# Loading the first head pair of queries and keys as f32 over the hardware queue, casting it on VectorE, and re-ordering the head of a fused attention and GEGLU kernel

## The chip, the cores and the metric

The kernel runs on one core of one Trainium2 chip. The metric is the device time of one execution in microseconds (us), as the median of several runs. Seven runs of the kernel before gave a median of 267.21 us, from 266.68 to 267.8 us.

The engines are called by the names of the profile: PE (TensorE matmul), PEld (TensorE weight load), DVE (VectorE), ACT (ScalarE), POOL (GpSimd) and SP (SyncE). PE, DVE and ACT each work through their own list of instructions in the order of the program. POOL issues the DMAs of the software queue [...], SP those of the hardware queue.

## What is computed

Inputs q, k and v have the shape (4 batches, 8 heads, 768 tokens, 64), in f32. Attention is sparse: a query sees the tokens less than 16 away, and besides them 24 block summaries, one for each block of 32 tokens. The output of attention goes through a GEGLU feed-forward part with a gated residual.

```python
k_sum = k.reshape(B, H, nb, block, D).max(axis=3)
v_sum = v.reshape(B, H, nb, block, D).mean(axis=3)
scores_l = where(|i - j| < 16, scale * q @ k.T, -1e9)
scores_s = scale * q @ k_sum.T + log(block)
a = softmax(concat([scores_l, scores_s]))
x = a @ concat([v, v_sum])              # heads side by side: (3072, 512)
ffn = (gelu(x @ w_gate) * (x @ w_val)) @ w_out
out = x + sigmoid(x @ w_res) * ffn      # d_ff = 1536
```

## The kernel before

Tokens are worked off in 8 units of 384 (half a batch each). A unit has an attention part and a feed-forward part. From unit to unit the two are interleaved: while the feed-forward part of unit u runs on PE, the scores and the attention of unit u+1 are woven in. The order of all instructions is written out by hand, and the loop over u (from L454) holds all of this. Only unit 0 has no feed-forward part to lie behind: its loads and its attention come first, alone, in the code of L124 to L160 (constants and loads) and L408 to L452. This piece is called the head here, and the change lies in it.

**The work of the head, by head pair.** There are four head pairs, hp = 0 to 3.

- `k_step` (L187) turns the keys of a pair on PE (16 small transposes at L183 into the PSUM tile `tp`), ACT copies them into the tile `kW` (L190), and `k_rest` (L194 to L203) makes five DVE instructions of them: two for the block maxima, two copies of the neighbouring tokens, one copy of the maxima.
- `q_step` (L205) turns the queries of a pair (8 transposes) and ACT copies them into `qT` (L207).
- `mask_step` (L249) writes the band mask into the PSUM tile `s` with two matmuls (L252), and `s_step` (L257) adds the scores on top with 12 small matmuls (L269). ACT takes the exponential (L278) into `P`. There is only one buffer for `s`, so that the mask of the next pair waits for the exponential of this one.
- `v_spread` (L235) are two DVE copies that lay the values out for odd tiles (L239, L242). `vsum_sum` (L221) sums values into block means with seven matmuls, one for each chunk of 128 tokens (L227); `vsum_out` (L231) copies the result out, two heads by DVE, six by ACT.
- `av_part` (L288) multiplies P with the values (L301): 12 matmuls with `blocks=False` for the tokens near by, 12 with `blocks=True` for the block means. `av_norm` (L304) divides by the row sum on DVE (L309, L311).
- `xt_step` (L313) turns the result for the feed-forward part: PE at L320, ACT copy at L322. The first feed-forward matmuls of unit 0 (tiles `gv`, `g`, `vv`, L333) follow.
- `keep_warm(n)` (L378) issues n matmuls on zeros (tile `wp`, L382) whose result nobody reads.

**Loads.** All loads of the head go over POOL's software queue in this order: keys of heads 0 to 3, queries of heads 0 to 3, keys of heads 4 to 7, queries of heads 4 to 7 (`load_tokens`, L85), then the seven chunks of the values (L96), then the weights `w_gate` and `w_val` in six slices each. Each has its type changed from f32 to bf16 on the way. Between them POOL makes masks with `select` (L115): `ident`, the bias, `maskt`, `bmean`. Eight of these DMAs may be under way at once; the ninth waits for the first.

**Order on PE in the head before:** 13 wp; k0, q0, k1, q1; mask, 3 wp, scores 0; k2, q2, mask, scores 1; k3, q3, mask, scores 2; value sums 0 to 2, 2 wp, mask, scores 3, 2 wp; value sums 3 to 6, each with 2 wp behind it (the last with 1); then near and block parts of pairs 0 and 1, then of 2 and 3; 3 wp; the turning of x.

**Order on DVE in the head before:** memsets of constants; `nmask` (L122), which needs `maskt` from POOL; memsets of `kW` and `vsum`; the four times five instructions of `k_rest`; the two `v_spread` copies; the copy out of the value sums; the norms.

Of the kernel before, what the change touches and what calls it, by code (L numbers as in the profile page):

```python
# [8 lines left out]
F32 = mybir.dt.float32  # L9
BF16 = mybir.dt.bfloat16  # L10
AF = mybir.ActivationFunctionType
# [4 lines left out]
def kernel(  # L16
# [11 lines left out]
    nc = tc.nc  # L28
    B, H, S, D = q.shape
# [12 lines left out]
    TU = S // 2  # L42
    NSUB = TU // 128
    NU = 2 * B
    NP = H // 2
    BAND = QT + 2 * WIN
    PP = 96

    const = ctx.enter_context(tc.tile_pool(name="const", bufs=1))
    wpool = ctx.enter_context(tc.tile_pool(name="wpool", bufs=1))  # L50
    qk = ctx.enter_context(tc.tile_pool(name="qk", bufs=2))
    work = ctx.enter_context(tc.tile_pool(name="work", bufs=3))
    ppool = ctx.enter_context(tc.tile_pool(name="ppool", bufs=4))
    upool = ctx.enter_context(tc.tile_pool(name="upool", bufs=2))
# [4 lines left out]
    MM, AO, TT, SS = (ps_mm, "mm"), (ps_o, "ao"), (ps_t, "t"), (ps_s, "s")  # L59
# [3 lines left out]
    NC = NT // 2  # L63
# [3 lines left out]
    bias_t = const.tile([128, 1], F32, name="bias_t")  # L67
    nmask = const.tile([128, QT], BF16, name="nmask")
    bmean = const.tile([128, NB - 2 + 128], BF16, name="bmean")
    pre = const.tile([1, 1], F32, name="pre")  # L70
# [9 lines left out]

    def token_tile(lo, hi, name):
        j = (hi - lo) // PP
        return qk.tile([PP, H, j, D], BF16, tag=f"{name}{j}", name=name)

    def load_tokens(t, src, b, lo, hi, h0, h1):  # L85
        j = (hi - lo) // PP
        nc.gpsimd.dma_start(  # L87
            out=t[:, h0:h1].rearrange("p h j d -> p h (j d)"),
            in_=src[b, h0:h1, lo:hi].rearrange("h (p j) d -> p h (j d)", j=j),
        )  # L90

    def load_values(b, c):

        lo, hi = (max(0, c * 128 - WIN), c * 128 + 128 - WIN) if c < NC else (S - WIN, S)
        dst = vext[b % 2][0 if c else WIN:128, 2 * c, :, 0:D] if c < NC else vext[b % 2][64:64 + WIN, NT - 1, :, 0:D]
        nc.gpsimd.dma_start(out=dst, in_=v[b, :, lo:hi, :].rearrange("h p d -> p h d"))  # L96

    k_sb, q_sb = {}, {}

    with tc.manual_schedule():  # L100

        def vext_consts(i):
            nc.vector.memset(vext[i][:, :, :, D:D + 1], 1.0)
            nc.vector.memset(vext[i][0:WIN, 0], 0.0)
            nc.vector.memset(vext[i][64:96, NT - 1], 0.0)
            nc.vector.memset(vext[i][64:64 + WIN, NT - 1, :, D:D + 1], 1.0)
# [7 lines left out]
        def select(ap, op, fill, base, step, cm):  # L114
            nc.gpsimd.affine_select(out=ap, in_=ap, compare_op=op, fill=fill, base=base,  # L115
                                    pattern=[[step, ap.shape[-1]]], channel_multiplier=cm)
# [9 lines left out]
        nc.vector.memset(bias_t[:], 0.0)  # L126
        nc.vector.memset(bias_t[96:128, :], logblk)
        nc.vector.memset(bmean[:], 1.0 / BLK)
        vext_consts(0)

        kt, qa, qb = token_tile(0, S, "k_sb"), token_tile(0, TU, "q_sb"), token_tile(TU, S, "q_sb")
        k_sb[0] = kt
        load_tokens(kt, k, 0, 0, S, 0, 4)
        select(ident[:], ALU.not_equal, 1.0, 0, -1, 1)
        load_tokens(qa, q, 0, 0, TU, 0, 4)
        load_tokens(kt, k, 0, 0, S, 4, 8)
        load_tokens(qa, q, 0, 0, TU, 4, 8)
        select(bias_t[96:128, :], ALU.is_ge, -30000.0, NB - 1, 0, -1)
        load_values(0, 0)
        mask_consts()  # L140
        kw_consts(0)
# [45 lines left out]
        def k_step(b, hp, pool, tag):  # L187
            tp = turn_pair(k_sb[b], hp, pool, tag)
            kw = kW[b % 2][hp]
            nc.scalar.copy(kw[:, :, OWN:OWN + QT].rearrange("d t (p j) -> d t p j", j=tp.shape[2]),  # L190
                           tp.rearrange("d (t p) j -> d t p j", t=NT))
            k_rest(kw)
# [12 lines left out]
        def q_step(src, b, lo, hi, hp, pool, tag):  # L205
            tp = turn_pair(src, hp, pool, tag)
            nc.scalar.copy(qT[b % 2][hp][:, lo:hi].rearrange("d (p j) -> d p j", j=tp.shape[2]), tp)  # L207
# [13 lines left out]
        def vsum_sum(b, pool, tag, chunks=range(NC + 1), vs=None):  # L221
            if vs is None:
                vs = pool.tile([128, DM], F32, tag=tag, name="vs")
            for c in chunks:
                lo = NB - 2 - 4 * c if c < NC else 0
                rows, t = (slice(0, 128), 2 * c) if c < NC else (slice(64, 64 + WIN), NT - 1)
                nc.tensor.matmul(vs[:], bmean[rows, lo:lo + 128], vext[b % 2][rows, t, :, 0:D],  # L227
                                 start=(c == 0), stop=(c == NC), skip_group_check=True)
            return vs
# [27 lines left out]
        def s_step(u, hp, st, s=None, two=None, masked=True):  # L257
            b, half = u // 2, u % 2
            first = s is not None
            if two:  # L260
                s = [pool.tile([128, 512], F32, tag=tag, name="s1") for pool, tag in two]
            elif not first:
                s = ps_s.tile([128, 2, 512], F32, tag="s", name="s")
            kw, qt = kW[b % 2][hp], qT[b % 2][hp]
            for t in range(HT):
                tt = half * HT + t
                for hh in range(2):
                    ps = slice(hh * 64, hh * 64 + 64)
                    nc.tensor.matmul((s[hh] if two else s[:, hh])[:, t * QT:(t + 1) * QT], kw[ps, tt, :],  # L269
                                     qt[ps, tt * QT:(tt + 1) * QT], start=not first, stop=True,  # L270
                                     skip_group_check=True)
            P = ppool.tile([128, 2, HT, QT], BF16, tag="P", name="P")
            if two:
                for hh in range(2):
                    nc.scalar.activation(P[:, hh].rearrange("p t q -> p (t q)"), s[hh][:, 0:TU], AF.Exp,  # L275
                                         scale=scale, bias=bias_t[:])
            else:
                nc.scalar.activation(P.rearrange("p a t q -> p a (t q)"), s[:, :, 0:TU], AF.Exp,  # L278
                                     scale=scale, bias=bias_t[:])
            st["P", hp] = P  # L280
            if not first and masked:
                mask_part(hp, st)
# [23 lines left out]
        def av_norm(hp, st):  # L306
            ao = st["ao", hp]
            rz = work.tile([128, NSUB, 2, 1], F32, tag="rz", name="rz")
            nc.vector.reciprocal(rz[:], ao[:, :, :, D:D + 1])  # L309
            xn = st["xn"].rearrange("p s (h d) -> p s h d", d=D)[:, :, 2 * hp:2 * hp + 2, :]  # L310
            nc.vector.tensor_mul(xn, ao[:, :, :, 0:D], rz.to_broadcast([128, NSUB, 2, D]))  # L311
# [66 lines left out]
        def keep_warm(n, wp=None):  # L378
            if wp is None:
                wp = ps_mm.tile([128, 512], F32, tag="mm", name="wp")  # L380
            for i in range(n):
                nc.tensor.matmul(wp[:], warm[:, 0:128], warm[:], start=True, stop=True)  # L382
# [24 lines left out]

        st = new_unit()  # L408
        wp = ps_o.tile([128, 512], F32, tag="ao", name="wp")
        keep_warm(13, wp)  # L410
        nc.scalar.activation(pre[:], bias_t[0:1, :], AF.Exp)
        for hp in range(2):
            k_step(0, hp, *MM)
            q_step(qa, 0, 0, TU, hp, *MM)
        s = mask_step()
        keep_warm(3, wp)
        s_step(0, 0, st, s)
        k_step(0, 2, *MM)
        q_step(qa, 0, 0, TU, 2, *MM)
        s = mask_step()  # L420
        s_step(0, 1, st, s)
        k_step(0, 3, *MM)
        q_step(qa, 0, 0, TU, 3, *MM)
        s = mask_step()
        s_step(0, 2, st, s)
        v_spread(0, 0, HT // 2, 0)
        v_spread(0, 0, HT // 2, 1)
        vs = vsum_sum(0, *MM, range(0, 3))
        keep_warm(2, wp)
        s = mask_step()  # L430
        s_step(0, 3, st, s)
        keep_warm(2, wp)
        for c in range(3, NC + 1):
            vsum_sum(0, *MM, range(c, c + 1), vs)
            keep_warm(2 if c < NC else 1, wp)
        vsum_out(0, vs, 0, 2, nc.vector.tensor_copy)
        vsum_out(0, vs, 2, 8, nc.scalar.copy)
        nc.scalar.activation(pre[:], bias_t[0:1, :], AF.Gelu)
        homes = (AO, TT, MM, MM)
        for p in (0, 2):  # L440
            for hp in (p, p + 1):
                av_part(0, hp, st, *homes[hp], blocks=False)
            for hp in (p, p + 1):
                av_part(0, hp, st, blocks=True)
                av_norm(hp, st)
        keep_warm(3)
        two = ps_s.tile([128, 2, 512], F32, tag="s", name="gv0")
        firsts = [(w_gate, 0, two[:, 0, :]), (w_val, 0, two[:, 1, :]), (w_gate, 1, None), (w_val, 1, None)]
# [5 lines left out]
        for u in range(NU):  # L454
# [6 lines left out]
            for fo in range(FO):  # L461
# [15 lines left out]
                if u == 1 and fo < 8:  # L477
                    home = TT if fo % 2 else AO
                    hp, kq = fo % NP, fo // NP
# [8 lines left out]
            if u == 0:  # L488
# [25 lines left out]
                st = nst  # L514
# [36 lines left out]
            st = nst  # L551
# [30 lines left out]
```

The softmax here doesn't subtract the row's maximum and nothing guards it: scores larger than these inputs give would overflow.

## Time and profile before

| | |
|---|---|
| median of 7 runs | 267.21 us (266.68 to 267.8) |
| the profiled execution's own time | 268.43 us |
| its span, first to last instruction | 266.7 us |
| mean granted TensorE clock | 0.992 |
| PE busy | 259.1 us (97% of the span) |
| DVE busy | 166.7 us (62%) |
| ACT busy | 139.0 us (52%) |
| POOL busy | 79.9 us (30%) |
| software DMA queue | 14.69 MB, its packets took 69.0% of 16 engines' span |
| hardware DMA queue | 9.44 MB, 15.1% |

The profiled execution took 268.43 us, of which 1.73 us lie outside the span. It is 1.22 us above the median of the timed runs. In a timeline, a line begins with the start and the duration of a group in us; "[1.11 <-DMA q_sb]" behind it says that the engine had stood idle for 1.11 us and what ended that. In a table of stretches, each engine has its busy time in the stretch with the number of instructions in brackets; behind them stand the granted TensorE clock (1.00 is full speed), the mean busy share of the DMA engines and the rate in GB/s.

### The profile page before, as it was taken

To read this page: it belongs to the slowest core of one execution; us is meant where nothing else is said; L and a number is where in the kernel's file an instruction comes from. 1 tells how busy PE (TensorE), PEld (TensorE's weight loads), DVE (VectorE), ACT (ScalarE), POOL (GpSimd) and SP (SyncE) were. 2 spreads that over 40 slices of the span, in tenths; PEclk is the share of its full clock that TensorE was granted. 3 is DMA by queue.
4 is the path that set the end of the run, shared out by engine and by line. 5 is a ranking of instruction groups with operands and counts; after the bars stand their busy time and mean duration, and the time that the engine had idled before them with its cause. 6 is when DMAs were issued, how large, how long until landed. Compare 5 with 4: busy or idle time off the path is not lost.

```text
span 266.7 us, 5841 instructions
## 1 busy us (share of the span) xinstructions
PE 259.1 (97%) x2330; PEld 145.6 (55%) x2330; DVE 166.7 (62%) x405; ACT 139.0 (52%) x240; POOL 79.9 (30%) x107
## 2 busy tenths in 40 slices
PE   8799999999999999999999999999999999999994
PEld 2446554556555555556655555556645565556543
DVE  3744762589486877478737867478737854674424
ACT  2755439657565533745365534744365636553310
POOL 7975633998999920040000000000000000000000
PEclk9979999999999999999999999999999999999999
DMA  6999999999999999448001355111001200020012
GB/s 83 171 169 196 197 206 186 147 161 190 127 125 149 183 131 141 76 63 119 0 2 41 97 102 91 31 54 66 0 2 43 79 0 2 11 105 6 2 39 79
DMA packets 90315, 24.50 MB, mean 92 GB/s; under 512 B 76464, under 2 KB 87344, under 8 KB 90288
## 3 DMA queue, kind: packets, MB, share of 16 engines
q0 software_dynamic: 73488, 14.69, 69.0%
q1 hardware_dynamic: 16800, 9.44, 15.1%
q8 instruction: 18, 0.29, 0.4%
q14 instruction: 9, 0.07, 0.1%
HBM read 29.36 MB, written 6.29 MB: 134 GB/s over the span
## 4 chain that ended last, share of the span: by engine, by line
PE 93%; DMA 3%; ACT 1%; POOL 1%; DVE 1%; issue 1%; POOLq 0%; DVEq 0%
PE f L367 23%; PE g L333 23%; PE vv L333 23%; PE r L351 8%; PE ao L301 4%; DMA q_sb<-in_q_dram 3%; PE vs L227 3%; PE s L269 3%; PE xp L320 2%; PE wp L382 1%; PE tp L176 1%; PE s L252 1%; PE gv L333 1%; POOL k_sb L87 1%; PE tp L183 0%
## 5 line engine op out<-in xcount | busy, mean ns | idle before, releaser
L333 PE MATMUL g<-xT,w_gate 128*128 128x384 bf16 x380 | 77.8, 326 | 0.0
L333 PE MATMUL vv<-xT,w_val 128*128 128x384 bf16 x380 | 77.8, 326 | 0.0
L339 ACT ACTIVATE ge<-g 128x384 f32<-128x384 f32 x95 | 46.6, 491 | 58.7 <-DVE gvT L340 32.4
L340 DVE TENSOR_TENSOR gvT<-ge,vv 128x384 bf16<-128x384 f32 x95 | 52.0, 552 | 36.8 <-PE vv L333 33.3
L367 PE MATMUL f<-w_out,gvT 128*128 128x512 bf16 (+2 forms) x312 | 69.5, 363 | 0.0
L333 PEld LDWEIGHTS <-w_val 128*128 128x128 bf16 x384 | 37.5, 98 | 25.4 <-issue 0.5
L333 PEld LDWEIGHTS <-w_gate 128*128 128x128 bf16 x384 | 36.9, 98 | 24.7 <-issue 0.8
L367 PEld LDWEIGHTS <-gvT 128*128 128x128 bf16 x312 | 27.6, 98 | 25.6
L96 POOL DMA_DIRECT2D vext<-in_v_dram x28 | 23.5, 882 | 22.1 <-DVE rz L309 22.1
L322 ACT COPY xT<-xp 128x384 bf16<-128x384 bf16 x32 | 15.0, 480 | 22.6 <-PE xp L320 22.6
L351 PE MATMUL r<-w_res,xT 128*128 128x512 bf16 x96 | 24.4, 380 | 0.0
L286 DVE TENSOR_TENSOR P<-P,maskt 128x768 bf16<-128x768 bf16 x28 | 15.6, 557 | 13.3 <-ACT P L278 10.2
L372 DVE SCALAR_TENSOR_TENSOR th<-th,f 128x512 f32<-128x512 f32 (+2 forms) x26 | 16.7, 641 | 11.4 <-PE f L367 8.5
L357 ACT ACTIVATE th<-r 128x512 f32<-128x512 f32 x24 | 14.2, 601 | 17.4 <-PE r L351 17.4
L166 POOL DMA_DIRECT2D k_sb<-in_k_dram x24 | 20.0, 863 | 10.7 <-DMA w_out<-in_moe_w_out_dram 5.2
L166 POOL DMA_DIRECT2D q_sb<-in_q_dram x24 | 19.8, 887 | 0.0
L311 DVE TENSOR_TENSOR xn<-ao,rz 128x384 bf16<-128x384 f32 x32 | 17.8, 557 | 1.1
L278 ACT ACTIVATE P<-s,bias_t 128x768 bf16<-128x768 f32 x18 | 16.2, 900 | 4.1 <-PE s L269 4.1
L374 DVE SCALAR_TENSOR_TENSOR o<-th,xn 128x512 f32<-128x512 f32 (+2 forms) x26 | 16.9, 651 | 0.9
L309 DVE RECIPROCAL rz<-ao 128x6 f32<-128x6 f32 x32 | 6.1, 190 | 18.0 <-PE ao L301 18.0
L275 ACT ACTIVATE P<-s,bias_t 128x384 bf16<-128x384 f32 x28 | 14.6, 577 | 0.0
L351 PEld LDWEIGHTS <-xT 128*128 128x128 bf16 x96 | 8.6, 98 | 8.5
(72 smaller groups left out, 207.1 us busy)
## 6 DMA issues: line engine op xcount, KB each, us to landing
out_dram<-o SPq DMA_DIRECT2D x23, 256.0 KB, 3.3
vext<-in_v_dram POOLq DMA_DIRECT2D x20, 128.0 KB, 6.2
k_sb<-in_k_dram POOLq DMA_DIRECT2D x24, 96.0 KB, 5.9
q_sb<-in_q_dram POOLq DMA_DIRECT2D x24, 96.0 KB, 5.1
w_gate<-in_moe_w_gate_dram POOLq DMA_DIRECT2D x6, 256.0 KB, 8.6
w_val<-in_moe_w_val_dram POOLq DMA_DIRECT2D x6, 256.0 KB, 8.7
w_out<-in_moe_w_out_dram POOLq DMA_DIRECT2D x3, 512.0 KB, 14.1
k_sb<-in_k_dram POOLq DMA_DIRECT2D x2, 384.0 KB, 6.1
```

The source lines that it names most:

```text
L96: nc.gpsimd.dma_start(out=dst, in_=v[b, :, lo:hi, :].rearrange("h p d -> p h d"))
L166: nc.gpsimd.dma_start(out=sb[b][:, h // 2, :, h % 2 * D:h % 2 * D + D], in_=src[b, h].rearrange("(c p) d -> p c d", c=NC))
L278: nc.scalar.activation(P.rearrange("p a t q -> p a (t q)"), s[:, :, 0:TU], AF.Exp, scale=scale, bias=bias_t[:])
L286: nc.vector.tensor_mul(Pf, Pf, maskt.unsqueeze(1).to_broadcast([128, 2 * HT, QT]))
L311: nc.vector.tensor_mul(xn, ao[:, :, :, 0:D], rz.to_broadcast([128, NSUB, 2, D]))
L333: nc.tensor.matmul(acc[:, 0:TU], w[:, ko, fs], st["xT"][:, ko, :], start=(ko == 0), stop=(ko == KO - 1))
L339: nc.scalar.activation(ge[:], g[:, 0:TU], AF.Gelu)
L340: nc.vector.tensor_mul(gvT[:, fo, :], ge[:], vv[:, 0:TU])
L351: nc.tensor.matmul(r[:], st["xT"][:, ko, ss], w_res[:, ko, :], start=(ko == 0), stop=(ko == KO - 1))
L367: nc.tensor.matmul(st["f", sub][:, 0:c1 - c0], gvT[:, fo, ss], w_out[:, fo, c0:c1], start=(fo == 0), stop=(fo == FO - 1))
L372: nc.vector.scalar_tensor_tensor(th, th, 1.0, f[:, 0:c1 - c0], ALU.add, ALU.mult)
L374: nc.vector.scalar_tensor_tensor(o[:, 0:c1 - c0], th, 0.5, st["xn"][:, sub, c0:c1], ALU.mult, ALU.add)
```

## The change

The keys of heads 0 and 1 and their queries of the first half are loaded as f32 by two DMAs of SP, into tiles `kf` (96 partitions x 1024) and `qf` (96 x 512). Two DVE copies cast them into the bf16 tiles. POOL loads heads 2 and 3 in the place of heads 0 to 3, keys and queries one behind the other, and makes `ident` after both. In the program, `vext_consts(0)` stands further down, but no other DVE instruction stands between the old and the new place, so that DVE's order is the same there. The two casts come on DVE behind the memset of `vsum`, which is the last of the constants.

On PE the queries of pair n+1 are turned after the scores of pair n, and the keys of pair n+1 before them. The near parts of pairs 0 and 1 come ahead of the last three value sums, those of 2 and 3 behind them, and all block parts and norms behind that. There are 15 wp where there were 27, not counting the 3 ahead of the turning of x, which stay. ACT loads the table for Gelu after the last exponential of the head, ahead of its copy of the value sums, and no longer behind it.

The order on PE is now: 8 wp; k0, q0, mask, 2 wp, k1, scores 0; 1 wp, q1, 1 wp, k2, mask, scores 1; 1 wp, q2, k3, mask, scores 2; q3, value sums 0 and 1, mask, scores 3; value sums 2 and 3, 2 wp, near parts 0 and 1, value sums 4 to 6, near parts 2 and 3, block parts 0 to 3; 3 wp; the turning of x.

```diff
+    qk1 = ctx.enter_context(tc.tile_pool(name="qk1", bufs=1))
...
-        return qk.tile([PP, H, j, D], BF16, tag=f"{name}{j}", name=name)
+        return qk1.tile([PP, H, j, D], BF16, tag=name, name=name)
...
         nc.vector.memset(bmean[:], 1.0 / BLK)
-        vext_consts(0)
-        kt, qa, qb = token_tile(0, S, "k_sb"), token_tile(0, TU, "q_sb"), token_tile(TU, S, "q_sb")
+        kt, qa, qb = token_tile(0, S, "k0"), token_tile(0, TU, "qa"), token_tile(TU, S, "qb")
         k_sb[0] = kt
-        load_tokens(kt, k, 0, 0, S, 0, 4)
+        kf = qk.tile([PP, 2, 8 * D], F32, tag="k_sb", name="kf")
+        qf = qk.tile([PP, 2, 4 * D], F32, tag="q_sb", name="qf")
+        nc.sync.dma_start(out=kf[:], in_=k[0, 0:2].rearrange("h (p j) d -> p h (j d)", j=8))
+        nc.sync.dma_start(out=qf[:], in_=q[0, 0:2, 0:TU].rearrange("h (p j) d -> p h (j d)", j=4))
+        load_tokens(kt, k, 0, 0, S, 2, 4)
+        load_tokens(qa, q, 0, 0, TU, 2, 4)
         select(ident[:], ALU.not_equal, 1.0, 0, -1, 1)
-        load_tokens(qa, q, 0, 0, TU, 0, 4)
         load_tokens(kt, k, 0, 0, S, 4, 8)
         load_tokens(qa, q, 0, 0, TU, 4, 8)
         select(bias_t[96:128, :], ALU.is_ge, -30000.0, NB - 1, 0, -1)
+        vext_consts(0)
         load_values(0, 0)
...
-        keep_warm(13, wp)
         nc.scalar.activation(pre[:], bias_t[0:1, :], AF.Exp)
-        for hp in range(2):
-            k_step(0, hp, *MM)
-            q_step(qa, 0, 0, TU, hp, *MM)
+        keep_warm(8, wp)
+        nc.vector.tensor_copy(kt[:, 0:2].rearrange("p h j d -> p h (j d)"), kf[:])
+        nc.vector.tensor_copy(qa[:, 0:2].rearrange("p h j d -> p h (j d)"), qf[:])
+        k_step(0, 0, *MM)
+        q_step(qa, 0, 0, TU, 0, *MM)
         s = mask_step()
-        keep_warm(3, wp)
+        keep_warm(2, wp)
+        k_step(0, 1, *MM)
         s_step(0, 0, st, s)
+        keep_warm(1, wp)
+        q_step(qa, 0, 0, TU, 1, *MM)
+        keep_warm(1, wp)
         k_step(0, 2, *MM)
-        q_step(qa, 0, 0, TU, 2, *MM)
         s = mask_step()
         s_step(0, 1, st, s)
+        keep_warm(1, wp)
+        q_step(qa, 0, 0, TU, 2, *MM)
         k_step(0, 3, *MM)
-        q_step(qa, 0, 0, TU, 3, *MM)
         s = mask_step()
         s_step(0, 2, st, s)
         v_spread(0, 0, HT // 2, 0)
         v_spread(0, 0, HT // 2, 1)
-        vs = vsum_sum(0, *MM, range(0, 3))
-        keep_warm(2, wp)
+        q_step(qa, 0, 0, TU, 3, *MM)
+        vs = vsum_sum(0, *MM, range(0, 2))
         s = mask_step()
         s_step(0, 3, st, s)
+        nc.scalar.activation(pre[:], bias_t[0:1, :], AF.Gelu)
+        vsum_sum(0, *MM, range(2, 4), vs)
         keep_warm(2, wp)
-        for c in range(3, NC + 1):
-            vsum_sum(0, *MM, range(c, c + 1), vs)
-            keep_warm(2 if c < NC else 1, wp)
+        av_part(0, 0, st, *AO, blocks=False)
+        av_part(0, 1, st, *TT, blocks=False)
+        vsum_sum(0, *MM, range(4, NC + 1), vs)
         vsum_out(0, vs, 0, 2, nc.vector.tensor_copy)
         vsum_out(0, vs, 2, 8, nc.scalar.copy)
-        nc.scalar.activation(pre[:], bias_t[0:1, :], AF.Gelu)
-        homes = (AO, TT, MM, MM)
-        for p in (0, 2):
-            for hp in (p, p + 1):
-                av_part(0, hp, st, *homes[hp], blocks=False)
-            for hp in (p, p + 1):
-                av_part(0, hp, st, blocks=True)
-                av_norm(hp, st)
+        av_part(0, 2, st, *MM, blocks=False)
+        av_part(0, 3, st, *MM, blocks=False)
+        for hp in range(NP):
+            av_part(0, hp, st, blocks=True)
+            av_norm(hp, st)
         keep_warm(3)
```

## The prediction

> **What bounds the kernel now.** I read the page's chain first: PE holds 93% of it, so a change in the head of the kernel pays only by making the first feed-forward matmul start earlier; from there on PE is busy nearly without a gap. So I then read the chain of waits of the first 30 us:
>
> ```profile
> 3.85 7.98 DMA q_sb<-in_q_dram
> ...
> 12.99 0.91 ACT P L278
> ...
> 15.17 1.39 PE vs L227 x3
> ...
> 17.66 0.54 PE wp L382 x2
> 18.20 0.22 PE vs L227
> ...
> 20.16 0.32 PE vs L227
> ...
> 20.85 2.07 PE ao L301 x95
> ...
> 24.41 0.48 PE gv L333 x2
> ```
>
> The reader is to see three pieces. To 11.87 the chain is the last query load. From 15.2 to 20.5 it is PE's own order: value sums and wp, while the scores of pair 3 are done at 17.67. From 20.5, the end of the value sums (call it T), to 24.41 it is attention, norms and the turning of x.
>
> Next DVE's timeline, since both casts are queued there:
>
> ```profile
> 6.14 0.78 DVE L122 TENSOR_SCALAR nmask<-maskt 128x64 bf16<-128x64 bf16 x1 [2.40 <-POOL maskt L115]
> ...
> 7.27 0.07 DVE L147 MEMSET vsum<- 32x8 bf16 x1
> ...
> 8.92 0.47 DVE L201 COPY kW<-kW 128x176 bf16<-128x176 bf16 x1
> ...
> 10.35 0.20 DVE L201 COPY kW<-kW 128x176 bf16<-128x176 bf16 x1
> ...
> 15.95 0.80 DVE L239 COPY vext<-vext 64x1536 bf16<-64x1536 bf16 x1
> 16.78 0.70 DVE L242 COPY vext<-vext 32x1536 bf16<-32x1536 bf16 x1
> ```
>
> DVE stands idle until POOL has made the mask, and is through its constants at 7.34. One and the same copy takes 0.20 or 0.47.
>
> Last the table of stretches, cut where the granted clock changes, and POOL's timeline:
>
> ```profile
> 6.35:9.76 3.41, 2.82 (x58) 1.60 (x58) 2.52 (x20) 2.30 (x4) 3.34 (x6) 1.00 1.30 192
> 9.76:13.17 3.41, 2.15 (x64) 1.46 (x66) 2.66 (x10) 2.25 (x4) 2.96 (x5) 1.00 2.64 153
> 13.17:16.58 3.41, 3.31 (x38) 1.60 (x33) 1.91 (x6) 2.69 (x4) 2.68 (x4) 0.50 3.29 142
> ```
> ```profile
> 7.60 4.07 POOL L96 DMA_DIRECT2D vext<-in_v_dram  x5
> ...
> 22.91 0.74 POOL L154 DMA_DIRECT2D w_val<-in_moe_w_val_dram  x1 [0.65 <-DMA w_val<-in_moe_w_val_dram]
> ```
>
> A stretch with PE busy for 2.15 of 3.41 us is followed by 3.41 us at half clock; one with 2.82 is not. POOL's line shows when the first slice of w_val has landed: 22.9.
>
> **The change, part by part.**
>
> *The loads over SP.* SP can issue at about 0.9, as the other engines start. Its nearest row is the output store: 256 KB, 3.3 us from issue to landing as a median, 2.0 in the quiet last 37 us. kf is 384 KB, so I take 4.5 to 5 for it and a little more for qf. In the bytes read from memory nothing changes; POOL's queue is relieved of two heads, so its later loads come no later. POOL still issues four loads and two selects ahead of `maskt`. The first two are half as large; a 16 KB load took 0.54 and a 384 KB one 0.67 to issue, so `maskt` comes 0.2 earlier at most. I take nothing.
>
> *The casts are not where the data is.* They stand behind `nmask`, so they begin at 7.3 although kf lies ready some 2.5 us before. This is the added wait, and all of k_rest, and through it ACT and PE, queue behind it. Their durations: by rows, the nearest copy SBUF to SBUF is L239, 1536 elements or 3072 bytes read per partition in 0.70 to 0.80; by bytes the k cast (4096 read) is 0.93 and q 0.5. The nearest f32 row, L374 with two operands, takes 0.65 for 512, which makes 1.2 and 0.65. [...] A copy is nearer to a copy than a two-operand operation, so I take 0.7 and 0.4[...].
>
> [...] I take 8.0 for k and 9.1 for q.
>
> *The head up to the scores of pair 3.* k0 is turned from 8.15 (6.66 before): 1.5 later. Transposes at half clock 0.6, ACT copy 0.80, k_rest about 1.5 beside POOL's issues (8.06 to 9.58 before): kW0 at 11.1. Scores 0 at 11.4; ACT has the copy of k1 ahead of the exponential: exponential 0 at 12.3, against 10.18 before. From here it no longer waits for q of heads 4 to 7 (landed at 11.83): the changed order needs k2 at about 13, q2 at 14.5. Each pair then costs: exponential 0.90, copies of q and k 0.48 and 0.80 on ACT, less overlap, about 2.0; k_rest 1.31 where POOL is quiet (11.80 to 13.11); mask 0.35, scores 0.30. So exponentials 1 to 3 at 14.4, 16.3 and 18.25 (12.99, 15.21, 17.71 before). Scores 3 end at 18.15, against 17.67: 0.5 late. The spread copies follow k_rest of pair 3 on DVE: 17.7 plus 1.5 is 19.2.
>
> *From there to T.* Before: 20.48 - 17.67 = 2.8 us. This piece loses 7 of its 9 wp and takes on one value sum (five for four). Now: value sums 2 and 3 (0.44), 2 wp (0.43), near parts of two pairs (24 of 95 matmuls of 2.07 us, 0.52) which may wait for the spread until 19.3, sums 4 to 6 (0.22+0.22+0.32). T is then 19.3 + 0.55 + 0.76 = 20.6, about the same as before. The last value load, issued at 11.1 with 6.8 to land, is there at 17.9: no bound.
>
> *From T to the first feed-forward matmul.* Before 24.41 - 20.48 = 3.93. Half of the near parts is done already; near parts 2 and 3 (0.5) cover the copy out of the value sums; block 0 from T+0.5 to T+0.75, blocks 1 to 3 after ACT's copy of the other six heads (DVE 0.30, then ACT 0.47) end at T+1.7; 3 wp 0.7; x of pair 0 turned at T+2.4, and from there to the matmul it takes what it took, 24.41 - 23.52 = 0.89: T+3.3. The norms, 0.69 a pair from T+0.9, give pair 1 at T+2.4, in time. So 0.6 is saved here. The Gelu table (1.28) lies behind exponential 3, 19.15 to 20.6, just ahead of ACT's copy: free, but if exponential 3 is later than 18.5 it becomes the late one.
>
> *The sum.* First matmul at 20.6 + 3.3 = 23.9 instead of 24.41: 0.5 us sooner. The weights allow 24.57 - 22.9 = 1.6. The later slices have more: the second slice of w_val had landed at 25.5 and is used at 28.1. So the 0.5 is kept. Behind unit 0 nothing changes. Profiled, 268.43 - 0.5 = 267.9; the median of the timed runs was 1.22 lower than the profiled time, so 267.21 - 0.5 = 266.7.
>
> *The fillers.* I costed the 12 lost wp as time won. They also carry the clock. After 8 wp (13 ended at 6.7, so 8 at about 4.7, 0.427 each) PE stands idle for 3.4 us and starts at half clock; that is in the transposes above. I let the clock rise at 13.2, as the cut of the stretches in this trace would have it. If it rises at 16.6 only, every pair costs 0.3 to 0.5 more and the gain shrinks to about 0.
>
> **The rivals.**
>
> *A, larger gain.* [...] the clock is full from 10 on: exponential 3 at 17.2, spread at 18.5, T at 19.8, first matmul at 23.1; 1.3 us, 265.9. The slack of the weights stops it at 1.6. For it: k_rest of 1.31 in quiet stretches. Against: five value issues stand just there.
>
> *B, slower.* The clock falls to half once more at the end of the head. Between 13.2 and 16.6 the new order has on PE two masks, 24 score matmuls, some 40 transposes, 1 wp and waits for ACT: about 2.8 of 3.41, at the edge between the two rows shown (2.15 falls, 2.82 does not). If it falls, what stands from 16.6 to 20 (seven sums at 0.2, mask, scores, near parts, 2 wp, together some 3.2) costs another 1.7, of which 0.4 lies in waits: 266.7 + 1.3 = 268.0. It decides as soon as PE is busy for less than some 2.5 us of such a stretch.
>
> *C, the change does not do what it says.* Casts [...] 1.2 + 0.65[...]: k0 not before 8.6, everything 0.5 to 0.9 later, 267.2 to 267.8. For it: no f32 copy in SBUF is in this trace.
>
> **How the numbers follow.** The forecast has 0.48, with its own range of 266.2 to 267.3; A 0.15, B 0.27, C 0.10. A measurement tells 0.2%, 0.53 us, from no change, so faster begins below 266.68. Of the forecast's 0.48, 0.25 is faster, 0.21 within, 0.02 slower; A is all faster, B all slower, C 0.03 within and 0.07 slower. Faster 0.40, within 0.24, slower 0.36. Range: A's and B's values with 0.1 to 0.3 on the outside, 265.8 to 268.3.
>
> **What would show it.** In the profile after: the k cast begins at 7.2 to 7.4 right behind the vsum memset, with kf landed long before; its duration (0.6 to 0.8, or 1.2); exponentials at 12.3, 14.4, 16.3 and 18.25; T near 20.6; the first gv matmul at 23.9; in the stretches no half clock after 16.6. I am wrong if the casts start near 5, if the half clock reaches into the near parts (B), or if the first matmul waits for w_val.

## The result, and the profile after

| | before | after |
|---|---|---|
| median | 267.21 us (61 executions) | 268.74 us (26 executions) |
| lowest to highest | 266.68 to 268.67 | 267.79 to 270.91 |
| ratio, 95% interval | | 1.0067 [1.0055, 1.0079] |
| the profiled execution's own time | 268.43 us | 267.87 us |
| its span | 266.7 us | 266.1 us |

The change makes the kernel slower: by 0.67% in the ratio, by 1.53 us (0.57%) in the medians. Yet the two profiled executions say the opposite: the one after is quicker by 0.56 us. Both are true, since the executions of either kernel differ by more than the change is worth, and the two that were profiled are not typical of theirs. The time of every execution is known, with its mean granted clock. Beside the kernels of the first experiments, the kernel before ran 58 times: 50 executions had a clock of 0.997 or more and took 266.8 to 267.7, and 8 had 0.991 to 0.994 and took 268.2 to 268.9. The trace in which the prediction was worked (0.992, 268.43) is of the second kind. The trace after (267.87) is close to the quickest of its 26, of which 16 took more than 268.5. (Ratios leave out executions over 1.5% above the quickest of their kernel, four in all of the runs below; medians and counts have them in.)

The chain of waits of the profiled execution after, to set against the first fence of the prediction:

```profile
7.29 0.70 DVE k L417
...
8.04 1.17 PE tp L188 x24
...
12.32 0.91 ACT P L283
...
14.32 0.90 ACT P L283
...
17.66 0.97 DVE vext L244
18.66 0.71 DVE vext L247
...
19.95 0.88 PE vs L232 x3
...
23.97 0.48 PE gv L338 x2
```

The wait for the query load is gone, and of the row of wp and value sums one block of three sums is left; the k cast and the ACT and DVE work of each pair carry the chain. The first feed-forward matmul comes at 23.97 instead of 24.41.

DVE's timeline shows where the casts stand, POOL's line what ran beside them:

```profile
6.09 0.78 DVE L123 TENSOR_SCALAR nmask<-maskt 128x64 bf16<-128x64 bf16 x1 [2.34 <-POOL maskt L116]
...
7.29 0.69 DVE L417 CAST k<-kf 96x1024 bf16<-96x1024 f32 x1
7.90 0.53 DVE L418 CAST qa<-qf 96x512 bf16<-96x512 f32 x1
```
```profile
6.90 1.25 POOL L116 TENSOR_SCALAR_AFFINE_SELECT bmean<-bmean 128x150 bf16<-128x150 bf16 x2
```

kf was issued at 0.8 and took 3.6 us, so it lay ready from 4.4 on, 2.9 us ahead of its cast. The two selects on POOL, which ran beside the casts here, took 1.25; before they took 0.70.

PE's timeline shows the idle time on which the rest of this document turns. In brackets is the idle time ahead of the group:

```profile
1.26 3.54 PE L387 MATMUL wp<-warm 128*128 128x512 bf16 x8 [1.26 <-DVE warm L125]
8.04 0.85 PE L188 MATMUL tp<-ident,k 96*64 96x96 bf16 x16 [3.24 <-DVE k L417]
```

### The profile page after: what moved, and what is told of

It reads as the page before. It is cut to its first block, busy times and chain, and to the rows that moved or that the text cites. A ratio compares the mean times of both kernels' runs of the same rounds, so it can differ in the third digit from the quotient of the medians.

```text
span 266.1 us, 5824 instructions
## 1 busy us (share of the span) xinstructions
PE 256.6 (96%) x2318; PEld 144.6 (54%) x2318; DVE 167.5 (63%) x407; ACT 139.0 (52%) x240; POOL 80.5 (30%) x107
## 4 chain that ended last, share of the span: by engine, by line
PE 91%; DVE 3%; ACT 2%; POOL 1%; issue 1%; POOLq 0%; DVEq 0%
PE f L372 23%; PE g L338 23%; PE vv L338 23%; PE r L356 8%; PE ao L306 3%; PE s L274 2%; PE vs L232 2%; PE xp L325 2%; PE tp L188 1%; PE tp L181 1%; ACT P L283 1%; ACT kW L195 1%; ACT qT L212 1%; PE wp L387 1%; PE gv L338 1%
## 5 line engine op out<-in xcount | busy, mean ns | idle before, releaser
L356 PE MATMUL r<-w_res,xT 128*128 128x512 bf16 x96 | 24.4, 380 | 0.0
L171 POOL DMA_DIRECT2D k_sb<-in_k_dram x24 | 19.9, 856 | 9.9 <-DMA w_out<-in_moe_w_out_dram 5.1
L280 ACT ACTIVATE P<-s,bias_t 128x384 bf16<-128x384 f32 x28 | 14.6, 578 | 0.0
## 6 DMA issues: line engine op xcount, KB each, us to landing
w_res<-in_moe_w_res_dram POOLq DMA_DIRECT2D x1, 512.0 KB, 12.3
```

The source lines that it names most:

```text
L171: nc.gpsimd.dma_start(out=sb[b][:, h // 2, :, h % 2 * D:h % 2 * D + D], in_=src[b, h].rearrange("(c p) d -> p c d", c=NC))
L356: nc.tensor.matmul(r[:], st["xT"][:, ko, ss], w_res[:, ko, :], start=(ko == 0), stop=(ko == KO - 1))
```

## The experiments

The granted clock has two values in these traces, 1.00 and 0.50, and between two of its changes lie 3.41 us (8.02 to 11.44 in the trace after, 13.17 to 16.58 in that of the prediction) or a multiple of it; these 3.41 us are called a step below. The theory to test, called theory 1 below: PE idles for 3.2 us behind 8 wp, and depending on where that falls against these steps, an execution spends much of the head at half clock. Rivals: the load over SP or the casts vary (2); fillers cost time wherever they stand (3); the new order itself costs (4). The kernel before was timed beside each of the others, and its row is the second.

| kernel | median us (lowest to highest, executions) | over 268.5 | ratio to before, 95% |
|---|---|---|---|
| the change | 268.74 (267.79 to 270.91, 26) | 16 | 1.0067 [1.0055, 1.0079] |
| the kernel before, beside those below | 267.36 to 267.39 in four groups (266.80 to 269.15, 144) | 12 | |
| 16 wp at the start | 267.36 (267.02 to 267.76, 22) | 0 | 0.9996 [0.9988, 1.0003] |
| 12 wp at the start | 268.30 (267.04 to 270.25, 22) | 11 | 1.0034 [1.0011, 1.0057] |
| 8 wp, later | 267.55 (267.10 to 271.37, 17) | 4 | 1.0015 [0.9996, 1.0034] |
| no wp at the start | 268.63 (268.12 to 271.42, 13) | 8 | 1.0052 [1.0028, 1.0075] |
| 8 wp, three for each single one | 269.76 (268.56 to 271.34, 8) | 8 | 1.0082 [1.0055, 1.0110] |
| 16 wp, no single ones | 267.37 (266.88 to 269.07, 22) | 4 | 1.0004 [0.9990, 1.0017] |
| casts early | 268.11 (265.61 to 270.03, 22) | 9 | 1.0008 [0.9986, 1.0029] |
| casts early, more wp | 266.16 (265.77 to 266.47, 5) | 0 | 0.9954 [0.9941, 0.9966] |
| casts and mask early, more wp | 266.25 (264.97 to 269.93, 14) | 1 | 0.9946 [0.9928, 0.9965] |
| before, 8 wp | 268.10 (267.06 to 268.76, 14) | 2 | 1.0014 [0.9999, 1.0029] |
| new order alone | 266.04 (265.98 to 266.09, 5) | 0 | 0.9951 [0.9938, 0.9963] |
| load and casts alone, 16 wp | 267.82 (267.71 to 268.66, 7) | 1 | 1.0025 [1.0013, 1.0036] |

**16 wp at the start.**

```diff
-        keep_warm(8, wp)
+        keep_warm(16, wp)
```

> The changed kernel with 16 wp ahead of the first keys' turn instead of 8, nothing else. Theory 1 (clock): the timed executions of the changed kernel spread from 267.8 to 270.9 because after 8 wp PE idles for 3.2 us and[...] runs the whole head at half clock in some executions. 16 wp at 0.427 us end at 8.1, when the casts are through, so the median should fall from 268.7 to about 266.8 and no execution lie above 268. Theory 2 (the load over SP or the casts vary from execution to execution): fillers change nothing, median 268.7 with the same spread. Theory 3 (the fillers cost time wherever they stand): 268.7 or slightly above.

Measured: 267.36, and the spread is gone: 22 executions within 0.74 us. Theory 1 stands, 2 and 3 fall: neither the load nor the casts were touched, and eight more matmuls that nobody reads made the kernel 1.4 us quicker. But 267.4, not the 266.8 expected: with its clock kept, the change is level with before. In its trace the 16 wp end at 7.3, not at 8.1, and the 0.87 us of idle time behind them did no harm that the times show.

**The casts ahead of nmask.** The two `tensor_copy` lines move into `mask_consts`, in front of `nmask`.

> The changed kernel with the two casts moved ahead of nmask on DVE, so that they follow the landing of kf (0.8 + 3.6 = 4.4 us) and not the constants. Nothing else changes, 8 wp as they are. Theory 1 (clock): PE starts the keys at about 5.2, right behind the 8 wp, so the 3.2 us of idle time goes; the median should fall by 1 to 3 us, to 266 to 267.5, and the profile should show the first exponential near 9.5 to 10 instead of 12.3. Theory 2 (the load over SP varies): the casts now hang on it directly, so the spread stays or grows and the median stays near 268.7.

Measured: 268.11, from 265.61 to 270.03. The quickest are where theory 1 put them and quicker than any execution of the kernel before; the median is not. Closing the gap to 0.59 us was not enough. In its trace (268.04) the clock did not rise during the 8 wp: the keys at 5.44 take 0.85 and the wp at 10.09 takes 0.61. By these durations and the step that ends at 20.81 it is full only from 10.57, and it is at half again for 3.41 us from 20.81, across the turning of x and the first feed-forward matmuls. Counted back from 10.57 in steps of 3.41, a step ends at 3.74 and cuts the wp in two.

**The kernel before with 8 wp.**

```diff
-        keep_warm(13, wp)
+        keep_warm(8, wp)
```

> The kernel before with 8 wp in place of 13 at the start, nothing else. Theory 1 (clock): PE idles from 4.7 to 6.6; the half clock reaches further into the head in part of the executions, so the time gets worse and spreads: median 267.5 to 268.5, single ones to 270. Theory 2 (the new load path is the cause): the kernel before has no such load, so 267.2 within 0.3 as before.

Measured: 268.10, with a ratio whose interval starts just below 1: a loss of the expected kind, 0.7 us by the medians, but not clear of noise. Its idle gap is 1.64 us (keys at 6.49), its other fillers are all there.

**No wp at the start.**

```diff
-        keep_warm(8, wp)
+        keep_warm(0, wp)
```

> The changed kernel with no wp ahead of the first keys' turn. Theory 1 (clock): PE is surely at half clock when the keys come, in every execution, so the profile should show what the slow executions of the changed kernel look like; median 268.5 to 270, less spread at the low end (few or none at 267.8). Theory 2 or 3 (load path, or fillers cost time): 268.7 or less, no worse than the changed kernel.

Measured: 268.63, lowest 268.12. As bad as with 8: the 3.4 us of wp that the change left at the start bought next to nothing.

**The change, a second profile.** No edit.

> The changed kernel once more, for one look at another execution. The trace that came with the result is of an execution near the fastest of 26 (267.87; the median is 268.74). Theory 1 (clock): about 4 in 10 executions are at half clock for most of the head; if this look is one of them its span is 268 to 269, its matmuls on zeros stay at some 0.6 us to 15 us or further, and the exponentials come 0.5 to 1 us apart more than in the first trace. If it is a quick one (266.1 to 267), nothing follows.

Measured: an execution of 270.0, span 268.3, clock 0.978. Cut where its clock changes (columns as before: PE, PEld, DVE, ACT, POOL, clock, DMA share, GB/s):

```profile
4.06:7.47 3.41, 0.47 (x2) 0.00 (x0) 1.25 (x15) 0.00 (x0) 3.16 (x8) 1.00 1.18 171
7.47:10.89 3.42, 2.86 (x32) 1.57 (x34) 2.05 (x7) 1.18 (x2) 3.42 (x5) 0.50 1.86 172
10.89:14.30 3.41, 2.94 (x54) 2.10 (x54) 1.54 (x7) 1.97 (x3) 3.41 (x5) 0.50 3.05 146
14.30:17.71 3.41, 3.41 (x43) 1.66 (x41) 1.27 (x5) 2.67 (x4) 3.03 (x5) 0.50 1.76 163
17.71:21.13 3.42, 3.15 (x44) 1.53 (x46) 2.89 (x7) 2.67 (x5) 2.35 (x5) 1.00 1.45 196
```

The quick execution, the one profiled with the result (267.87), cut in the same way:

```profile
4.61:8.02 3.41, 0.19 (x1) 0.00 (x0) 1.79 (x16) 0.00 (x0) 3.21 (x7) 1.00 1.25 190
8.02:11.44 3.42, 3.40 (x44) 2.08 (x44) 1.68 (x6) 1.18 (x2) 3.42 (x5) 0.50 2.32 158
11.44:14.85 3.41, 3.22 (x71) 1.88 (x69) 1.87 (x7) 3.20 (x5) 3.41 (x6) 1.00 3.43 136
```

In both, the clock rises during the 8 wp, at 4.06 and 4.61 (in that of 270.0 the last wp takes 0.38, the first six 0.61 to 0.63; in the quick one the last takes 0.58, those ahead of it 0.63), and it falls one step later, behind a step that holds next to nothing of PE's work (0.47 and 0.19 us). What differs is when it comes back. The keys are turned at 8.03 and 8.04. In the quick execution a step begins just there, PE is busy for 3.40 us of it, and the clock is full again at 11.44. In the other the step begins 0.56 us ahead of the keys, PE is busy for 2.86, and half clock stays for two more. Two other traces agree: without wp at the start a step begins at 8.35 and the clock is full at its end (11.76, by the duration of the matmuls); with three wp for each single one it begins at 7.78, and the clock is still at half at its end (full from 14.6). PE's timeline of the execution of 270.0:

```profile
13.49 0.85 PE L188 MATMUL tp<-ident,k 96*64 96x96 bf16 x16
14.28 0.82 PE L257 MATMUL s<-nmask,ident 128*128 128x384 bf16 x2
15.03 0.50 PE L274 MATMUL s<-qT,kW 64*128 64x64 bf16 x12
...
25.64 0.32 PE L338 MATMUL gv<-xT,w_gate 128*128 128x384 bf16 x1 [0.40 <-ACT xT L327]
```

The pair that took 0.53, 0.48 and 0.35 in the quick execution takes 0.85, 0.82 and 0.50, and the first exponential, at 12.33 in both, is the last thing on which they agree. The first feed-forward matmul comes 1.67 us later. The clock is the only difference seen: the casts stand at 7.29 and 7.89 in this trace too.

**Early casts, with wp where PE waited.** On top of the early casts: 10 wp at the start, 4 ahead of the first mask, 5 behind the keys of pair 1, 1 ahead of scores 2, 4 ahead of the near parts.

> The casts ahead of nmask on DVE, and wp put where PE waited in the look at that kernel: 10 instead of 8 at the start, 4 ahead of the first mask, 5 instead of 2 between the keys of pair 1 and the scores of pair 0, 1 ahead of scores 2, 4 instead of 2 ahead of the near parts. Theory 1 (clock): the early casts are worth about 1.7 us once the clock is kept up, which the fastest execution without these fillers showed (265.6); median 265.2 to 266.0, spread under 1 us. Theory 3 (fillers cost time wherever they stand): ten more of them at 0.21 us make it 2 us slower than the 268.1 of the early casts alone.

Measured: 266.16, all five within 0.7. The same casts, which spread over 4.4 us, are now steady and 0.46% quicker than before.

**The new order alone.** The loads and 13 wp of the kernel before, the changed lines from the first mask on.

> One part of the change alone: the loads, casts and constants of the kernel before (software queue, 13 wp at the start), with the changed order of PE, ACT and DVE behind the first queries and its fewer fillers. Theory 1 (clock and start gap are the whole loss): keys start at 6.66, so the head gains what the new order saves; 266 to 267, with a few executions above 268 as in the kernel before. Theory 4 (the new order itself costs, the load does not): 268 or more, as the change as a whole.

Measured: 266.04. In PE's timeline:

```profile
6.62 0.53 PE L183 MATMUL tp<-ident,k_sb 96*64 96x96 bf16 x16
...
21.80 0.32 PE L333 MATMUL gv<-xT,w_gate 128*128 128x384 bf16 x1 [0.40 <-ACT xT L322]
```

Theory 4 falls: the order is the good half of the change.

**The load and casts alone.** The changed loads with 16 wp, and behind them the order and fillers of the kernel before.

> The other part alone: the f32 load over SP and the two casts where the change has them, 16 wp ahead of the keys so that PE does not idle, and behind that the order and the fillers of the kernel before. Keys start at 8.2 instead of 6.6. Theory 1: no clock loss, only the later start, part of which lay in the wait for q of heads 4 to 7 at 11.87: 267.3 to 268.3. Theory 4: the load is harmless, 267.3 within 0.2.

Measured: 267.82, 0.25% slower. The keys are turned at 8.03, 1.4 to 1.6 us later than in the traces before, of which the old order hides two thirds; in the traces before it waited for the last query load (11.24 and 11.87), here it does not.

**The kernel before, a second profile.** No edit.

> The kernel before once more, for a look at another execution. Of its timed executions 50 of 58 show a mean clock of 0.997 or more and take about 267.3; the trace the prediction was made from (0.992, 268.43) belongs to the other 8. Theory 1 (the prediction read an unusual execution): this look is one of the 50, has no half clock after the first 7 us, its value sums at 15 us take 0.22 us each and the first feed-forward matmul comes at about 23.3 instead of 24.41. Otherwise the baseline of the prediction was right and the loss lies elsewhere.

Measured: 267.26, clock 0.998, span 265.6. PE's timeline:

```profile
14.01 0.83 PE L227 MATMUL vs<-vext,bmean 128*128 128x512 bf16 x3
...
23.13 0.32 PE L333 MATMUL gv<-xT,w_gate 128*128 128x384 bf16 x1 [0.40 <-ACT xT L322]
```

The three value sums that took 1.46 in the prediction's trace take 0.83, and the first feed-forward matmul comes at 23.13. Its clock is full from 5.30 to 264.7. By its time and clock this is the typical kernel before, and the trace after (23.97) loses 0.84 us against it.

**8 wp, but later.** The memset of the zeros moves behind that of maskt, so that the wp run from 3.79 to 7.4.

> The changed kernel with its 8 wp at the start moved, not multiplied: the memset of the zeros they read stands behind the memset of maskt on DVE, so that they run from about 4 to 7.4, right up to the keys' turn, and PE's idle time lies ahead of them. Theory 1a (it is the idle gap right before the keys): as with 16 wp, median 267.4, none above 268. Theory 1b (it is the length of the busy stretch[...]): the spread stays, median 268.3 to 269.

Measured: 267.55, 13 of 17 below 268.1, but 4 above 268.5. Mostly 1a: as many fillers as in the change, with the idle time ahead of them and 0.64 us behind them, repair most executions. Not all: 16 wp left none above 268.5.

**12 wp at the start.**

```diff
-        keep_warm(8, wp)
+        keep_warm(12, wp)
```

> The changed kernel with 12 wp at the start, 5.1 us of them, and 1.7 us of idle time up to the keys. Theory 1b [...]: in between, median 267.5 to 268.2, a part of the executions above 269. Theory 1a (any gap of more than a us loses the clock): 268.7 as with 8. Theory 3 (fillers do not matter): 268.7.

Measured: 268.30, half of the executions above 268.5. The median lies just above the 267.5 to 268.2 of 1b. Whether it is the length or the gap, this run does not tell; but 8 late wp with 0.64 us behind them lost fewer (4 of 17), so the gap seems to count for more. And the clock rose without a whole step of wp: the one that ends at 4.06 in the second profile of the change held 2.80 us of them. In the trace here (269.88) the clock is full from 6.07 (the last wp takes 0.45, those ahead of it 0.63) and falls at 9.48, behind a step that held the 1.66 us of idle time.

**Casts and mask early.** On top of the early casts with wp, POOL makes `maskt` behind `ident`, and `nmask` and the `kW` memsets come ahead of the casts; 2 wp ahead of the first mask.

> The best version that the runs so far point to: early casts and the added fillers, and POOL's maskt ahead of the loads of heads 4 to 7, so that nmask and the other constants are done before kf lands and no longer stand between the casts and the first k_rest; 2 instead of 4 wp ahead of the first mask. Theory 1: first exponential at 9.0 instead of 9.9, but k of heads 4 to 7 lands at 10 to 11 and q at 12 and bounds the next pairs; 265.5 to 266.2, level with or a little below the new order alone (266.04).

Measured: 266.25, the lowest 264.97, with one execution of 269.93. The best single times of all, but not steadier or quicker in the median than the new order alone. In its trace k2 waits 0.32 us for the load of heads 4 to 7, as expected.

**Three wp for each single one.**

```diff
-        keep_warm(1, wp)
+        keep_warm(3, wp)
```
(three places)

> The changed kernel with each of the three single wp between the pairs made three; the 8 at the start and the gap behind them stay. If the start gap decides alone, the spread stays as it is, median 268.7, and all executions bear six more fillers (up to 1.3 us). If the lost fillers between the pairs are what keeps the clock down once it has fallen, the slow executions get shorter: median 267.8 to 268.4 and few above 269.5.

Measured: 269.76, no execution below 268.5. Half clock lasted two steps (6.83 us) in its trace (269.89) instead of the three of the change's second profile, but the wp, some of them at half clock and ahead of work that is waited for, cost more than that gave back. The gap is not repaired further down.

**16 wp and no single ones.** The three `keep_warm(1, wp)` go, with 16 at the start.

> The changed kernel with 16 wp at the start and none of the three single ones between the pairs. If the start gap decides alone: as with 16 wp and the single ones, 267.2 to 267.4, no spread. If those between the pairs are needed too, executions above 268.5 come back.

Measured: 267.37, 4 of 22 above 268.5, against none of 22 with the single ones. In its trace (268.51) the clock is at half from 12.89 to 19.71. The start's share is the large one; that the single wp keep the clock in some executions is likely, but four executions do not show it.

## Why the prediction was wrong

**What held.** In the one trace after, these steps came within 0.3 us: casts at 7.29 (7.3 predicted), the k cast 0.69 (0.7), exponentials at 12.32, 14.32, 16.39 and 18.16 (12.3, 14.4, 16.3, 18.25), the end of the spread at 19.37 (19.2), T at 20.83 (20.6), the first feed-forward matmul at 23.97 (23.9), the span 0.6 us shorter (0.5). Not so the clock: the prediction let it rise at 13.2, and it was full at 11.44. The 13.2 came from the cuts of the trace before (6.35, 9.76, 13.17), and those belong to that one execution: in the two of the change they stand at 4.61, 8.02, 11.44 and at 4.06, 7.47, 10.89.

**The base.** The step that failed first is the last of the sum: "the median of the timed runs was 1.22 lower than the profiled time, so 267.21 - 0.5 = 266.7". It took the 1.22 for a constant. It was the mark of an unusual execution. Of 58 executions 8 had the mean clock that goes with the 0.50 of 13.17 to 16.58 (0.991 to 0.994); the typical one, in its second profile, has none of it and comes to the first feed-forward matmul at 23.13, so that the sum should have been 23.9 - 23.1 = 0.8 slower, or 268.0, which is about what the quick executions after take (267.8 to 268.2). The sign was wrong before any further loss of clock. The warning stood on the table: the profiled execution lay outside the range of the seven timed ones, 266.68 to 267.8.

**The fillers.** The other term that failed. "I costed the 12 lost wp as time won. They also carry the clock." The second sentence was right and too small: for a late rise of the clock the prediction had the gain shrink to about 0, that is a first matmul near 24.4. It came at 25.64 in the second profile, and 16 of 26 took more than 268.5. The median lies 0.87 us above the profiled 267.87, which was where the prediction had put it (267.9): with the 1.22 of the base this makes up the whole 2.04 us between 266.7 and 268.74, to 0.05. Rival B was given 0.27 and placed at 16.6 to 20; the half clock ran from 7.47 to 17.71, right out of the gap. Its test, PE busy for less than some 2.5 of 3.41 us, fails as well. With early casts:

```profile
17.40:20.81 3.41, 2.92 (x95) 2.04 (x96) 1.36 (x4) 1.96 (x3) 2.42 (x5) 1.00 1.44 194
20.81:24.22 3.41, 3.16 (x29) 1.74 (x22) 2.22 (x7) 0.86 (x2) 2.13 (x3) 0.50 1.45 197
```

With 8 wp, but later:

```profile
7.60:11.01 3.41, 2.13 (x44) 1.33 (x44) 2.31 (x7) 1.98 (x3) 3.41 (x5) 1.00 1.93 162
11.01:14.42 3.41, 3.07 (x76) 2.08 (x77) 1.96 (x7) 2.80 (x5) 3.41 (x6) 1.00 3.96 136
```

With 12 wp at the start:

```profile
12.89:16.31 3.42, 3.42 (x50) 1.96 (x51) 1.41 (x7) 2.09 (x4) 3.42 (x6) 0.50 2.26 144
16.31:19.72 3.41, 3.41 (x38) 1.51 (x34) 2.02 (x6) 2.40 (x4) 2.76 (x5) 0.50 1.38 183
```

The clock fell behind 2.92 and stood behind 2.13. It stayed at half behind 3.42, though in the second profile of the change 3.41 brought it back at 17.71. So the busy time of this table, from which some of PE's records may be missing, does not by itself say what the clock will do.

The stretches at half clock here are 3.41, 6.83 and 10.24 us long, and the cuts lie elsewhere in each execution although the first wp starts at 1.26 in both profiles of either kernel. Against the 267.36 of 16 wp, the 8 wp cost 1.4 us in the median (268.74, 0.5%), which is most of the 1.53 lost, and 3.5 us in the slowest execution (270.91, 1.3%). A gap shorter than a step went with the loss too: with 1.66 us of idle time behind 12 wp the clock fell in the trace (at 9.48), and half of the executions took more than 268.5.

**Where the time went, in sum.** The new order is worth 266.04 - 267.39 = -1.35 us. The load, cast where the change casts it, takes it back: 267.36 - 266.04 = +1.32, with the clock kept (keys turned at 8.19 instead of 6.62 in the two traces). The lost fillers ahead of the keys take another 268.74 - 267.36 = +1.38. The last two sums compare kernels that were not timed beside each other, while the kernel before moved from 267.21 to 267.39; that 0.18 is what the three lack of the 1.53 measured. The +1.32 holds all in which 16 wp and the new order alone differ: the loads, the casts and three wp.

**Smaller points.** The 0.7 and 0.4 of the prediction for the casts were the author's estimate; they lie between what L239 (1536 elements in 0.70 to 0.80) gives by elements, 0.5 and 0.25, and by bytes, 0.93 and 0.5. Measured were 0.69 and 0.53, so rival C with its 1.2 fell. That the q cast ends only at 9.1 was an estimate too, which no row of the trace showed: it ended at 8.43. The times beside POOL are not steady: 0.69 and 0.53 for the casts in the trace after, with 1.25 for POOL's two selects, 0.85 and 0.78 for the casts with 16 wp. What sets them was not measured. The w_val slack of 1.6 was misread: the issue at 22.91 is the twelfth of the weights and stood 0.65 us until the fourth, the second slice, had landed. In the same way the first of the weights, at 12.11, stood 0.45 us until the load eight ahead of it, the last of the queries, had landed. In the trace after, the first slice of w_val had landed at 19.9, 4.2 us ahead of its use, and PE waited for no weight. One more reading was wrong, without harm to the sum: from 11.80 to 13.11 POOL was not quiet but issued two weight loads (at 12.11 and 12.87). And of the two copies of L201, that of 0.20 at 10.35 ran, like that of 0.47 at 8.92, beside POOL's five value issues (7.60 to 11.67).

**What stays open.** Why four of 17 executions with 8 late wp, and one with early casts and mask, still took more than 268.5, was not settled. Six of the 26 executions of the change, the slowest (270.36 to 270.91), have a mean clock of 1.000, and none of them was profiled. The trace without wp at the start reads 1.000 too, with its matmuls at half clock up to 11.76, so a late first rise would explain them; it is not shown. Which of PE's work sets the clock was not measured by itself. That the order together with a load that arrives early would beat the order alone is not shown: 266.16 and 266.25 against 266.04.

## What to carry to other kernels

A profile is one execution: before a saving is worked out in it, its own time must be set against the range of the timed runs, and a stretch at half clock in it, and the moments at which its clock changes, belong to that execution until the others are known to have them (13.17 to 16.58 at half clock in one profile of the kernel before, none of it in the other). Data that arrives early wins nothing when the engine that unpacks it works in order and stands behind an earlier wait (kf lay ready at 4.4 and was cast at 7.29, behind a wait of 2.34 us for POOL): move the unpacking with the load. Fillers ahead of a wait are not free to go (8 wp in place of 16 cost 1.38 us here); when data is expected sooner, they may only be cut once it is seen to be used sooner.

## What the runs showed of the hardware

In the table of stretches the clock reads 1.00 until its first recorded change, also where PE runs at half clock: the first wp last 0.63 us in a stretch that reads 1.00, where later ones have 0.38, and one at 12.96 in the second profile of the change, where it reads 0.50, has 0.61. The duration of a known matmul is the surer sign. In the profile of 12 wp and in the second one of the change, half clock lasted 10.24 us, three times 3.41, although PE counted as busy for 9.2 of them. In the traces that record more than one change, the changes lie whole multiples of 3.41 us apart (13.17, 16.58 before; 8.02, 11.44 after; 7.47, 17.71 in the second profile of the change), and where they start differs from execution to execution of the same kernel (6.32 and 5.30 in the two of the kernel before).
